# Relu-squared attention and a GELU feed-forward in one kernel: fourteen output stores issued by ScalarE instead of SyncE, one more gate on GpSimd, and a new instruction order in the middle

## The chip, the cores and the metric

The kernel runs on one core of one Trainium2 chip. The metric is the device time of one execution in microseconds (us). The core has TensorE (PE in the profile; PEld is its weight load), VectorE (DVE), ScalarE (ACT), GpSimd (POOL) and SyncE (SP), which work at the same time and wait for each other by semaphores. Transfers are issued from the queues of SP, ACT and POOL and carried out by 16 DMA engines.

## The reference

```python
B, H, S, D = 8, 12, 448, 64
scores = q @ k.transpose(0, 1, 3, 2) / sqrt(D)        # per batch and head
attn   = maximum(scores, 0) ** 2 / S
x      = (attn @ v).transpose(0, 2, 1, 3).reshape(3584, 768)
h      = x @ w_in                                     # w_in  768 x 2048
g      = 0.5 * h * (1 + erf(h / sqrt(2)))
out    = g @ w_out                                    # w_out 2048 x 768
```

All inputs and the output are float32 in memory.

## The kernel before

**The work.** There are eight batches of 448 tokens. A batch goes through attention in three groups of four heads. For each group and each of seven blocks of keys there is one step: four matmuls for the scores (`ps`, L741, 64x64 tiles of the array), a relu with scaling to bf16 (L753 on ACT or L755 on DVE), and a square (L762 on DVE). After seven steps a set of 28 matmuls multiplies by v (`pav`, L802), and two copies bring the result to `xT` (L511 on DVE, L513 on ACT).

The feed-forward has two layers. The first (`psh`, L854) takes `xT` times `w_in`, six matmuls of 448 columns for 128 hidden units, then one GELU on ACT (L864). For the last three batches it is done in blocks with sums of blocks and fewer products (`pb`, L998, L1035, L1044). The second layer goes over groups of 256 tokens, numbered 0 to 13. Each group has seven products of eight matmuls of 384 columns (`pso`, L1171), which are put together on DVE and ACT (L1205, L511, L513) in two tiles `osb` of 128 x 768, the two halves of the group. Each half is written to memory by two DMA transfers (L1132), because the rows of the output are split over two places there. There are three `osb` buffers, three PSUM buffers for attention and two for the feed-forward.

**How q and k come in.** For batches 2 to 7, POOL loads k, q and v with a cast to bf16 (L546, L467, L564). SP then transposes q and k by DMA: nine transfers `DMA_TRANSPOSE` for each batch (L660), three for each group of heads: one of k and two of q. I call them T(b,0) to T(b,8) for batch b. The first score matmul of batch b needs T(b,0), T(b,1) and T(b,2). T(b,...) may be issued when the loads of batch b have landed and when the scores of batch b-2 are done, because there are two buffers. The loads of the next batch overwrite what the transposes read. So POOL holds them back with a "gate", a tiny copy that reads the transposed data (L701 and L709): a gate behind T(b,2), one behind T(b,6), then the load of v of batch b itself, a gate behind T(b,8), then six loads of k and q of batch b+1. The v load of the last batch stands right behind its six loads of k and q.

**What sets the order.** Every piece of work is registered with `Scheduler.add`, with the engines that can do it, its planned length and the pieces that it needs. The string `ORDER` (L83 to L163) then names the pieces one by one with a letter for the engine (P, A, D, G for POOL, S for SP) and the number of the piece. `Scheduler.place` sends them to their engines in that order, so `ORDER` fixes what each engine does and in which order. POOL's pieces also stand in the list `pool_q`, which is only followed for what `ORDER` leaves out; `ORDER` leaves out nothing here.

**The queues.** In the order of instructions, each DMA issued by SP or ACT takes the next of eight landing semaphores, in the order of `ORDER`. Before it is issued, its engine waits until the transfer eight places before it has landed, since that one had the same semaphore. SP carries both the transposes and the stores in one in-order queue. ACT issues two loads at the start and two small stores at the end.

The lines that the prediction's steps touch are: L660 (transposes, SP), L1132 (stores), L701, L709, L564 (gates and v load, POOL), L741 (scores), L802, L854, L998, L1171 (the other sets on PE), L864 and L753 (ACT), L1205 (DVE into `osb`).

Of the kernel before, what the change touches and what calls it, by code (L numbers as in the profile page):

```python
# [15 lines left out]
HC = NC // 2  # L16
HS = S // 2
# [76 lines left out]
A260 D182 D187 P263 D215 A211 D188 P261 G151 A205 P207 A264 P216 S230 G153 D206 D185 D224 A262  # L94
A217 P192 A208 G154 D193 D194 D209 D212 P247 D221 A248 P255 P143 D218 A256 P201 P225 A144 A226
G237 D202 D203 P265 D227 D380 S231 D386 S232 P245 S233 A266 P362 A246 P372 A363 P370 A373 A371
D390 D388 P356 P366 A357 P368 A367 P376 D389 A369 A377 P358 P364 D383 D381 A359 A365 P360 P350
A361 P354 A351 P288 P282 D387 D384 A355 A289 P294 P378 A295 P374 P276 S234 A379 G240 D283 D284
D382 G149 P279 A375 P291 D280 D385 S235 P348 P352 P285 A292 A277 A349 D296 D290 D286 D287 A353
P306 P303 S236 P392 P300 D393 A304 P342 P394 D395 P396 P398 D391 A307 D281 A343 P312 P315 G152  # L100
A397 A301 A313 G155 G242 D278 D293 D316 G269 P297 G270 D399 G271 G272 P327 P400 D298 P402 D314
D302 D427 P324 A299 A328 S408 P309 D401 D403 P336 P404 A325 S409 A310 A337 P431 D305 D317 D326
G273 P318 A432 P339 P333 P435 D428 A334 G274 S410 D405 D311 P433 S411 S406 A340 P447 D319 A448
D344 D308 P462 D320 P321 G417 D434 P330 D429 P437 A322 A436 D329 D430 D335 A331 D341 P439 A323
S412 D338 D332 S413 P459 A463 P453 P345 A454 D460 D438 D440 S414 S415 P474 P465 D475 D455 G420
P441 P443 D442 A346 A466 P486 D444 A347 D467 G275 S416 P450 D451 A487 P456 D452 P531 G423 A532
D570 P547 A548 P549 P545 A550 D457 D571 S407 A546 P498 D464 P489 P504 D449 P529 D461 P523 A499
A490 P477 G418 D458 P480 D505 D478 A530 G419 P468 S551 G421 S552 A481 P471 A524 D476 D482 D469
D472 P483 D572 D473 P527 A484 S445 D488 P537 A528 P533 D506 P510 G422 D485 A470 A538 D491 A534
P507 P501 S553 D500 A511 G424 P539 A502 A508 G425 S554 P519 P625 G560 A626 P513 D479 A520 P492  # L110
P495 D514 D512 S555 P616 S556 S557 A540 D493 D515 P525 D496 A617 A494 G563 P535 P619 S558 D509
A526 D627 G426 S559 P613 A536 D614 G566 P610 P543 A544 D615 P541 D503 P521 D497 D573 G561 P640
A620 A611 P646 A641 D647 P516 D517 P634 A522 A542 D642 S446 P628 P574 A635 D629 P576 G562 P670
D612 S714 D621 D630 A518 S715 G564 P622 D618 G565 A575 P664 A623 A671 P578 D577 P580 P661 P637
A665 D624 D581 A638 P631 P649 D662 P676 A579 S716 D639 P582 P584 A632 D633 P652 A677 D583 A650
P667 D636 A653 D585 S588 D651 S717 D648 A668 D654 P643 A644 G567 P586 S718 D590 P594 P779 D645
D587 P673 P655 A780 G568 D592 D591 A595 P658 A674 P596 P782 D666 A659 S589 S719 D597 P773 A783
P598 A774 P600 D656 S720 P815 D663 P785 D675 A599 D657 P776 D669 D672 A786 G723 A777 A816 D601
G726 D660 D775 P602 D678 P604 P809 D735 D593 P791 S721 D603 D605 P679 A810 P806 P606 S722 D781
A680 S608 D778 P692 D607 D681 D792 A807 G569 A693 P706 P788 D787 P797 P824 A707 P686 A687 P704  # L120
D789 D790 G729 P702 D784 G724 P830 A798 S877 D793 A825 D817 P812 P794 G725 D831 A705 P803 A813
A795 D804 P836 D805 S878 S609 A703 G727 G728 A837 P708 A796 S879 D814 S880 P712 P833 D808 P839
D811 D733 P800 A709 P682 D801 A713 D802 D826 D799 A834 S881 A683 P700 G730 G731 D840 P696 A701
P688 S882 P925 P934 A935 P818 A689 D926 A697 P922 D832 P821 A819 P694 D734 D736 D923 D841 A820
G886 A695 A822 P710 S883 A711 D823 P827 P940 D828 G889 P931 D835 D829 P698 S884 A941 A699 D838
P690 A932 P684 D927 P919 G732 A691 P928 A685 D920 P842 D924 D936 A929 S885 P916 A843 A917 P949
P737 G892 G887 P739 D930 A950 P955 G888 D921 D844 S988 P943 S989 D933 G890 G891 A738 A956 D740
D918 D944 P964 P741 P743 A742 P745 D744 A965 D942 D746 P747 P749 P952 D753 D951 P946 S990 D748
# [4 lines left out]
P865 A1001 P849 A866 A1037 P857 P1006 D972 P1024 D1002 A850 D969 P985 A1025 P1009 D1007 A858 P1012  # L133
D1077 P875 P869 A876 P861 A1013 S996 D897 A870 D986 A862 P873 D899 A874 A987 D1038 D1010 P847 S771
P1057 A848 P1030 P1003 D1008 D1011 A1031 P853 D1069 D1058 A1004 P863 D1014 P1063 D1029 D1005 A864
P1018 P1021 A854 D1064 P1045 P859 A1022 A1019 D1032 D1073 A860 D1074 P845 P867 P1039 D1070 A1046
A846 A1020 D1023 D1078 A868 P1051 P1033 P851 A1034 D1035 A852 A1040 P902 D1026 D1047 P900 A1052
D1065 P1048 A901 D1041 D1053 D1059 P1060 A1061 D903 P1042 P1054 A1043 A1049 D1079 D1080 P904 A905
D1044 D1071 P906 D1062 A1055 P908 P1081 D1151 D907 S772 D909 D1056 P1083 P1098 A1099 P1100 D1076
P912 P910 D1149 D1150 A1082 D1050 P1066 D913 D911 S914 D1084 S915 P1085 D1072 D1101 P1153 A1067  # L140
A1068 P1102 A1154 D1075 P1087 D1152 P1104 A1086 D1189 P1089 A1103 D1190 P1106 D1088 P1155 D1105
D1090 P1092 D1107 A1091 D1191 P1109 A1108 D1156 P1095 P1112 D1093 P1115 D1110 A1094 P1132 D1096
A1111 P1117 D1113 A1097 P1134 D1192 A1116 A1133 P1157 A1114 D1118 P1119 D1135 P1136 A1158 P1121
P1138 A1120 P1123 A1137 P1140 D1122 P1159 D1139 D1124 P1126 D1141 A1125 P1143 A1142 D1160 P1129
P1146 D1127 P1161 D1144 A1128 D1130 A1145 P1163 D1147 A1131 D1301 A1148 D1162 D1302 P1165 D1169
D1164 S1167 P1173 D1170 D1166 S1168 P1175 D1171 D1174 P1177 D1172 D1176 D1303 P1179 D1304 A1178
P1181 D1180 P1183 D1263 D1182 P1185 D1261 D1184 S1187 P1193 D1262 P1210 D1186 S1188 P1195 D1264
P1212 A1194 A1211 P1265 D1196 P1197 D1213 P1214 A1266 P1199 P1216 A1198 P1201 A1215 P1218 D1200
P1267 D1217 D1202 P1204 D1219 A1203 P1221 A1220 D1268 P1207 P1224 D1205 P1227 D1222 A1206 P1244
D1208 A1223 P1229 D1225 A1209 P1246 A1228 A1245 P1269 A1226 D1230 P1231 D1247 P1248 A1270 P1233  # L150
P1250 A1232 P1235 A1249 P1252 D1234 P1271 D1251 D1236 P1238 D1253 A1237 P1255 A1254 D1272 P1241
P1258 D1239 P1273 D1256 A1240 D1242 A1257 P1275 D1259 A1243 A1260 D1274 P1277 D1281 D1276 S1279
P1285 D1282 D1278 S1280 P1287 D1283 D1286 P1289 D1284 D1288 P1291 D1290 P1293 D1292 P1295 D1375
D1294 P1297 D1373 D1296 S1299 P1305 D1374 P1322 D1298 S1300 P1307 D1376 P1324 A1306 A1323 P1377
D1308 P1309 D1325 P1326 A1378 P1311 P1328 A1310 P1313 A1327 P1330 D1312 P1379 D1329 D1314 P1316
D1331 A1315 P1333 A1332 D1380 P1319 P1336 D1317 P1339 D1334 A1318 P1356 D1320 A1335 P1341 D1337
A1321 P1358 A1340 A1357 P1381 A1338 D1342 P1343 D1359 P1360 A1382 P1345 P1362 A1344 P1347 A1361
P1364 D1346 P1383 D1363 D1348 P1350 D1365 A1349 P1367 A1366 D1384 P1353 P1370 D1351 P1385 D1368
A1352 D1354 A1369 P1387 D1371 A1355 A1372 D1386 P1389 D1393 D1388 S1391 P1397 D1394 D1390 S1392
P1399 D1395 D1398 P1401 D1396 D1400 P1403 D1402 P1405 D1404 P1407 D1415 D1406 P1409 D1413 D1408  # L160
S1411 P1417 D1414 D1410 S1412 P1419 D1416 D1418 P1421 D1420 P1423 D1422 S1433 P1425 D1424 P1427
D1426 S1434 P1429 D1428 S1435 P1430 D1431 S1436 D1432 S1437
# [232 lines left out]
def kernel(  # L395
# [300 lines left out]
    def add_gate(b, g):  # L696
# [438 lines left out]
    def add_group(g):  # L1135
# [79 lines left out]
        def store(x, c, queues):  # L1215
            return lambda e: store_rows(rows[x][0] // 128, osb(x), c, queues)
# [295 lines left out]
```

## Time and profile before

| what | value |
|---|---|
| device time, median of 3 runs (range) | 368.6 us (368.53 to 369.44) |
| device time of the profiled execution | 368.77 us |
| span of the profiled execution, first to last instruction | 367.0 us |
| granted TensorE clock | 0.998 |
| PE busy | 356.0 us, 97% |
| DVE busy | 286.4 us, 78% |
| ACT busy | 201.5 us, 55% |
| POOL busy | 63.7 us, 17% |
| DMA traffic | 47.25 MB |

The profiled execution took 1.8 us more than its span, which is time before its first and after its last instruction. Between 30 us and 250 us, PE is busy 217.64 of 220 us, ACT 142.08 and DVE 184.17. The chain that ended last goes by engine through PE for 80%, DMA for 8%, SP's queue for 5% and ACT for 4%.

How to read what follows: a line of a timeline has the start, the length, the engine, the line of the kernel and the operation, the tile that it writes and the tiles that it reads, the count, and in brackets the idle time of the engine before it and what ended that. "SPq" is SP's own queue: the time of such a line is the issue of a transfer, not the transfer. "us to landing" runs from the issue to the last byte's notice. In the chain of waits, each row is one stretch with its start, its length and who held the end up.

### The profile page before, as it was taken

The page shows a single profiled execution, that of the slowest core. Times are in us where ns is not written, and L with a number is a line of the kernel's source. Part 1 is how long each engine was busy: PE and PEld are TensorE (multiplying, and loading weights), DVE is VectorE, ACT ScalarE, POOL GpSimd, SP SyncE. Part 2 cuts the span into 40 slices and gives each one's busy share as a digit, 9 for nine tenths or more (in the row PEclk, how much of TensorE's full clock was granted, in tenths as well). Part 3 has the DMA queues.
Part 4 walks back from the last instruction along what each step waited for, and adds up shares of the span by engine and source line. Part 5 has one row for each costly group of instructions (what it writes and reads, how often), then busy time and mean ns, then how long its engine had stood idle before and what let it go on. Part 6 is the DMA issues. An engine that isn't in the chain of part 4 may idle for free.

```text
span 367.0 us, 8384 instructions
## 1 busy us (share of the span) xinstructions
PE 356.0 (97%) x3517; PEld 218.4 (60%) x3517; DVE 286.4 (78%) x480; ACT 201.5 (55%) x319; POOL 63.7 (17%) x103
## 2 busy tenths in 40 slices
PE   7899999999999899999999999999999999999995
PEld 3566465455544455554455544467886897688663
DVE  3998886389899787888997798799778558755863
ACT  4997754676757576748672656763540353045200
POOL 8665700160140240150150000000000000000000
PEclk9999999999999999999999999999999999999999
DMA  9999999999999999999899950002002301210232
GB/s 169 199 202 204 202 204 179 189 171 204 173 169 207 161 180 193 187 182 201 167 179 163 235 127 2 0 2 70 18 2 88 86 2 36 94 46 0 87 87 86
DMA packets 89700, 47.25 MB, mean 129 GB/s; under 512 B 55360, under 2 KB 86336, under 8 KB 89664
## 3 DMA queue, kind: packets, MB, share of 16 engines
q0 software_dynamic: 32912, 22.47, 42.0%
q1 hardware_dynamic: 56112, 23.76, 33.4%
q8 instruction: 27, 0.44, 0.5%
q10 hardware_dynamic: 640, 0.51, 0.4%
q14 instruction: 9, 0.07, 0.1%
HBM read 45.61 MB, written 11.01 MB: 154 GB/s over the span
## 4 chain that ended last, share of the span: by engine, by line
PE 80%; DMA 8%; SPq 5%; ACT 4%; issue 1%; DVE 1%; DVEq 0%; POOLq 0%; POOL 0%; ACTq 0%
PE pso L1171 32%; PE psh L854 20%; PE pb L998 13%; PE ps L741 8%; PE pav L802 7%; DMA qT<-nq 5%; SPq L660 4%; ACT a_sq L753 3%; DMA nk<-in_k_dram 2%; DMA k<-in_k_dram 1%; SPq L1132 0%; PE tp L605 0%; ACT kT L513 0%; ACT xT L513 0%; DVE a_sq L762 0%
## 5 line engine op out<-in xcount | busy, mean ns | idle before, releaser
L753 ACT ACTIVATE a_sq<-ps 128x896 bf16<-128x896 f32 (+1 forms) x122 | 106.8, 921 | 31.4 <-PE ps L741 31.1
L762 DVE TENSOR_TENSOR a_sq<-a_sq 128x896 bf16<-128x896 bf16 (+1 forms) x169 | 96.4, 614 | 2.8 <-ACT a_sq L753 2.4
L854 PE MATMUL psh<-xT,win_sb 128*128 128x448 bf16 (+1 forms) x516 | 95.7, 340 | 0.0
L854 PEld LDWEIGHTS <-win_sb 128*128 128x128 bf16 x516 | 48.2, 98 | 45.1 <-issue 8.9
L755 DVE TENSOR_SCALAR a_sq<-ps 128x896 bf16<-128x896 f32 (+1 forms) x47 | 50.6, 1076 | 20.6 <-PE ps L741 20.6
L1171 PEld LDWEIGHTS <-s_sb 128*128 128x128 bf16 x456 | 43.4, 98 | 29.9 <-issue 3.5
L864 ACT ACTIVATE h_sb<-psh 128x448 bf16<-128x448 f32 x80 | 43.3, 547 | 30.6 <-PE psh L854 30.4
L741 PE MATMUL ps<-qT,kT 64*64 64x448 bf16 (+1 forms) x756 | 47.6, 336 | 3.9 <-DMA qT<-nq 1.9
L1035 DVE TENSOR_TENSOR part<-pb,part 128x448 f32<-128x448 f32 x60 | 34.7, 619 | 21.0 <-PE pb L998 21.0
L1171 PEld LDWEIGHTS <-h_sb 128*128 128x128 bf16 x336 | 32.0, 98 | 23.2 <-issue 3.5
L1171 PE MATMUL pso<-wout_sb,h_sb 128*128 128x384 bf16 x224 | 41.1, 326 | 0.0
L1171 PE MATMUL pso<-wout_sb,s_sb 128*128 128x384 bf16 (+2 forms) x232 | 41.1, 321 | 0.0
L1171 PE MATMUL pso<-t_sb,s_sb 128*128 128x384 bf16 x224 | 41.0, 326 | 0.0
L802 PE MATMUL pav<-a_sq,v_sb 64*64 64x448 bf16 (+1 forms) x756 | 36.6, 329 | 0.3 <-ACT a_sq L753 0.2
L1205 DVE TENSOR_TENSOR osb<-pso,p_sb 128x384 f32<-128x384 f32 x42 | 23.3, 554 | 15.2 <-PE pso L1171 11.2
L741 PEld LDWEIGHTS <-kT 64*64 64x64 bf16 x756 | 18.4, 105 | 25.3 <-issue 19.9
L1044 ACT ACTIVATE h_sb<-part 128x448 bf16<-128x448 f32 x36 | 20.1, 578 | 20.2 <-DVE part L1035 19.9
L998 PEld LDWEIGHTS <-win_sb 128*128 128x128 bf16 x288 | 27.6, 98 | 2.3 <-issue 0.4
L802 PEld LDWEIGHTS <-v_sb 64*64 64x64 bf16 x756 | 21.5, 107 | 11.3 <-issue 1.2
L513 ACT CAST xT<-pav 128x448 bf16<-128x448 f32 (+1 forms) x31 | 15.3, 509 | 11.5 <-PE pav L802 9.8
L998 PEld LDWEIGHTS <-ws 128*128 128x128 bf16 x216 | 20.7, 98 | 0.0
L1171 PE MATMUL pso<-t_sb,h_sb 128*128 128x384 bf16 x112 | 20.5, 326 | 0.0
(60 smaller groups left out, 264.7 us busy)
## 6 DMA issues: line engine op xcount, KB each, us to landing
nk<-in_k_dram POOLq DMA_DIRECT2D x23, 224.0 KB, 8.5
nq<-in_q_dram POOLq DMA_DIRECT2D x21, 224.0 KB, 9.3
v_sb<-in_v_dram POOLq DMA_DIRECT2D x5, 672.0 KB, 10.0
out_dram<-osb SPq DMA_DIRECT2D x7, 336.0 KB, 3.6
v_sb<-in_v_dram POOLq DMA_DIRECT2D x9, 224.0 KB, 8.0
out_dram<-osb SPq DMA_DIRECT2D x7, 288.0 KB, 3.3
out_dram<-osb SPq DMA_DIRECT2D x8, 240.0 KB, 3.1
win_sb<-in_moe_w_in_dram POOLq DMA_DIRECT2D x8, 192.0 KB, 8.5
```

The source lines that it names most:

```text
L741: nc.tensor.matmul(ps[64 * j : 64 * j + 64, e, x * w : x * w + w], kT[r, g, i * 128 + 64 * j : i * 128 + 64 * j + 64], moving, start=True, ...
L753: A.activation(ar, ps, AF.Relu, scale=c_att)
L755: V.tensor_scalar(ar, ps, c_att, 0.0, op0=mybir.AluOpType.mult, op1=mybir.AluOpType.max,)
L762: V.tensor_mul(box["a2"][:, :, :used], ar, ar)
L802: nc.tensor.matmul(pav[0][o2 : o2 + 64, e, :w], vt[b][r, 2 * g + e, bass.ts(i, D)], box["a2"][r, y, o : o + w], start=(i == 0), stop=(i == ...
L854: nc.tensor.matmul(ph[:, x * n : x * n + n], win_sb[:, kd, bass.ts(m + x, 128)], xT[b][:, kd, c], start=(kd == 0), stop=(kd == KD - 1),)
L864: A.activation(h_ring()[:, m : m + nm, o + c.start : o + c.stop], box[0][:, :S].rearrange("p (x n) -> p x n", x=nm), AF.Gelu,)
L998: nc.tensor.matmul(bank[name][:, y, z * HS : z * HS + HS], w[:, k, bass.ts(mm, 128)], right()[:, k], start=first and k == 0 and z == 0, st ...
L1035: V.tensor_add(get(to), ps(name), get(other))
L1044: A.activation(h_ring()[:, m : m + 2, o + half[c].start : o + half[c].stop], src().rearrange("p (x n) -> p x n", x=2), AF.Gelu,)
L1171: nc.tensor.matmul(box[bank][:, n0:n1], left()[:, kf], right()[:, kf, n0:n1], start=bool(need) and kf == 0, stop=kf == K2 - 1, skip_group_ ...
L1205: V.tensor_add(out()[:, n0:n1], box[bank][:, n0:n1], other()[:, n0:n1])
```

## The change

There are three edits. First, the stores of groups 0 to 6 of the second layer (two halves of two transfers each, 28 transfers) are registered for ACT and issued on ACT's queue; the stores of groups 7 to 13 stay on SP. Second, a function `add_vgate` registers a small copy on POOL that reads transposed q of batch 7 and needs T(7,5); it is registered last, as piece 1441. Third, `ORDER` is new from batch 1's attention to the blocks of batch 5 (the first 72 entries of PE and its last 124 are the same). The number of pieces of each kind stays the same on PE. ACT has 14 store pieces more, two relus fewer and five copies fewer; DVE has these seven more.

```diff
+ACT_STORES = 7
...
-A260 D182 D187 P263 D215 A211 D188 P261 G151 A205 P207 A264 P216 S230 G153 D206 D185 D224 A262
+D224 D215 G151 P247 A260 A211 A248 D187 P265 A205 P192 D182 P216 D185 P207 D217 A266 P245 D206
...
-D953 P937 D750 A947 G893 D954 P982 P958 D754 P757 A758 P759 P761 D957 S751 S991 D938 A959 A983
-P997 A939 D960 P973 A998 D755 P979 G894 D760 D948 S992 P763 A762 A974 P765 D966 D764 D999 P767
-P967 S752 S993 D756 D766 D945 P976 A980 S994 A977 D975 D968 P961 P1015 A1016 P1027 D768 D896 D1028
-P769 D770 P871 D962 S995 G895 P855 D898 D981 D978 A872 A963 P970 D971 A856 D1017 P1036 D984 P1000
...
+D918 P745 G891 D923 A950 D753 P743 D924 D744 G893 P958 P982 A947 A959 G894 G895 P937 P979 D983
+P976 D754 A977 D938 A980 D746 S990 P747 D748 A939 P749 S991 D948 D750 P757 D755 P952 P1003 S992
+D960 S993 S994 A758 A752 P943 A1004 P759 D942 D756 D953 P761 D760 P763 A762 D984 D764 D978 P765
...
+D975 A860 A1016 A1034 G1441 S996 P964 P869 D965 D966 P847 P1009 P1030 D969 D1014 A1010 P985 D1031
...
+    def add_vgate(b):
+
+        def fn(e):
+            nc.gpsimd.tensor_copy(gate, get_T(b)[0][:, 32 * KC : 32 * KC + 16])
+
+        pool_q.append(sch.add((("POOL", 0.2, 0.3),), fn, [Tq[b, 1, 1][0]]))
...
         if g < NG - 1:
-            sch.add((("SP", 0.6, 2.8),), store(1, full, [nc.sync] * 2), [c22, c21], frees=("osb",))
-            sch.add((("SP", 0.6, 2.8),), store(0, full, [nc.sync] * 2), [c11] + c12, frees=("osb",))
+            queue, eng = (nc.scalar, "ACT") if g < ACT_STORES else (nc.sync, "SP")
+            sch.add(((eng, 1.0, 2.8),), store(1, full, [queue] * 2), [c22, c21], frees=("osb",))
+            sch.add(((eng, 1.0, 2.8),), store(0, full, [queue] * 2), [c11] + c12, frees=("osb",))
...
+    add_vgate(B - 1)
     sch.run({"PE": pe_q, "POOL": pool_q})
```

In these lines S988 to S996 are T(7,0) to T(7,8), G893 and G894 the last loads of k and q of batch 7, G895 its load of v, G1441 the new gate, S751 and S752 the two stores of group 4, the second of which becomes A752.

More of the change, by code (lines that the diff above doesn't have):

```diff
@@ L99 @@
[L99 to L128, printed above, removed]
@@ L159 @@
[L159 to L162, printed above, removed]
+D224 D215 G151 P247 A260 A211 A248 D187 P265 A205 P192 D182 P216 D185 P207 D217 A266 P245 D206
+P263 A193 S230 A208 D209 A246 P255 G153 A264 D218 D221 P261 D194 G154 A256 A262 D188 P201 D212
@@ new lines @@
+S231 D380 S232 P225 P143 A202 A203 S233 D381 A226 A227 P376 A144 P370 S234 D383 A377 D388 P368
+G237 A371 G240 P358 A369 D384 P348 G149 D389 A359 A349 P378 P356 A379 A357 P372 A373 P362 A363
+G152 D386 D385 D387 P350 P360 A351 A361 G155 P364 P285 A365 P291 D292 P279 S235 A286 S236 P352
+P294 A280 P288 D390 A353 P276 A277 P354 P366 A355 P303 D295 D289 G242 A367 D287 P282 A283 P306
+P374 D296 P392 D281 D278 G269 A304 A375 G270 P330 P318 D307 P342 A393 P394 A319 D391 A343 P396
+P336 G271 D284 S408 D293 D305 D290 A331 D395 P309 S409 G272 P297 D337 P312 S410 A310 D382 A298
@@ new lines @@
+D397 P300 P398 D332 A299 A301 D320 D311 S411 A313 G273 D344 P400 D399 P315 S412 D427 A316 P333
+G274 P324 D401 P402 D314 P404 A325 D403 P431 A406 D302 D317 D308 P327 D428 P321 S413 D432 D405
+A328 D429 D322 P339 P433 G417 S414 D329 A334 A340 D341 A323 P462 G420 G275 S415 P465 S416 D335
+A463 D326 A466 G423 P453 D434 A454 D464 D338 D430 P435 G418 P437 P459 P450 P345 D438 D460 D436
+P456 A451 G419 S551 P483 A346 D484 P439 P441 P474 D347 A457 P495 D440 P447 D452 D572 A496 P443
+P480 D475 D442 D444 A448 D455 P471 P504 P529 A472 D485 D458 D461 G421 P545 A530 P525 A505 G422
@@ new lines @@
+A546 D467 P547 P477 S552 D449 P468 A481 P501 D506 S553 A526 D478 A548 D570 D476 A445 D502 P486
+P539 A469 D479 D487 G424 P531 A540 A532 P535 D497 A407 P549 P489 P510 S554 A536 D470 G425 D488
+P498 S555 P533 D503 A550 D511 D499 D482 A534 P519 S556 A490 P537 D473 D491 A520 P507 P492 A538
+D508 D509 P513 P622 P521 A514 G560 S557 D512 A623 P527 A522 D493 G563 D500 S558 A494 P610 P652
+D515 S559 A528 A611 P516 D571 G426 D612 P625 G566 A653 D624 D626 P543 A544 P523 P541 A517 A524
+A542 G561 A518 D627 P574 D575 P576 G562 D577 P619 P640 P616 A620 S714 D617 A641 G564 P578 P628
@@ new lines @@
+P613 P649 P580 G565 S715 G567 D654 D629 A614 A650 S716 D642 D581 D621 P634 G568 D630 D651 A579
+P673 P646 D615 A446 S717 A647 D618 P582 A635 P584 D585 D583 P670 S718 A674 P631 P637 A671 S719
+P643 G723 D573 A638 A644 D636 D592 D590 D591 D648 D645 P594 S720 D639 P586 S721 D587 P676 A595
+A588 A677 A632 P598 P596 D593 P661 A633 A662 P776 G726 P655 D678 D597 P788 D777 D599 D663 D789
+P791 P600 G569 A656 P602 D601 S722 P604 D672 A657 P785 D675 A792 D603 P667 P664 P606 G729 D668
+P658 G724 A786 D605 P782 A665 P779 D607 G725 D793 D787 A608 G727 P696 D783 A659 A697 P712 D669
@@ new lines @@
+A780 P688 A713 D666 P824 D660 D825 P773 P679 P812 A689 P694 G728 D781 A813 D778 A695 P706 D680
+P684 P797 A774 A707 P815 D681 P800 S877 D784 A685 S878 P702 S879 D735 D733 A816 A801 D826 D775
+D790 A703 D798 P698 P692 P806 P809 A693 G730 D802 D807 G731 A810 A699 P794 D817 P803 D808 D814
+P821 P710 A822 S880 D795 S881 P690 A711 D796 A804 G886 P925 A691 S882 S883 D799 P836 D811 A926
+P830 P708 D837 A589 D805 D734 P686 A831 P833 P827 A828 A687 P818 D834 A709 S884 G889 G732 P928
+S885 A609 A819 D832 D835 P839 D929 P700 P704 G892 P934 A840 D820 P970 D829 A701 G887 P919 A705
@@ new lines @@
+A1037 D1076 D1053 A866 P902 D1062 A901 P904 D1071 A1058 D1059 D1077 A1082 P1085 P1021 D1074 A772
+A1022 D903 D1038 P1066 P1024 P1098 A1067 P906 A905 A1025 D1078 D1023 D1068 D1075 D907 P908 P1083
+P1100 D1151 D1189 A1099 D1026 D1190 P1042 P910 D1149 D1084 P1102 D1101 D1043 D909 D1072 D1044 P912
+D911 D1150 P1089 P1087 P1104 A914 P1153 D913 D1152 A1103 P1106 A915 A1086 A1154 D1080 D1088 P1155
+D1105 D1090 P1092 D1107 A1091 D1191 P1109 A1108 D1156 P1095 P1112 D1093 P1115 D1110 A1094 P1132
+D1096 A1111 P1117 D1113 A1097 P1134 D1192 A1116 A1133 P1157 A1114 D1118 P1119 D1135 P1136 A1158
@@ new lines @@
+P1121 P1138 A1120 P1123 A1137 P1140 D1122 P1159 D1139 D1124 P1126 D1141 A1125 P1143 A1142 D1160
+P1129 P1146 D1127 P1161 D1144 A1128 D1130 A1145 P1163 D1147 A1131 D1301 A1148 D1162 D1302 P1165
+D1169 D1164 S1167 P1173 D1170 D1166 S1168 P1175 D1171 D1174 P1177 D1172 D1176 D1303 P1179 D1304
+A1178 P1181 D1180 P1183 D1263 D1182 P1185 D1261 D1184 S1187 P1193 D1262 P1210 D1186 S1188 P1195
+D1264 P1212 A1194 A1211 P1265 D1196 P1197 D1213 P1214 A1266 P1199 P1216 A1198 P1201 A1215 P1218
+D1200 P1267 D1217 D1202 P1204 D1219 A1203 P1221 A1220 D1268 P1207 P1224 D1205 P1227 D1222 A1206
@@ new lines @@
+P1244 D1208 A1223 P1229 D1225 A1209 P1246 A1228 A1245 P1269 A1226 D1230 P1231 D1247 P1248 A1270
+P1233 P1250 A1232 P1235 A1249 P1252 D1234 P1271 D1251 D1236 P1238 D1253 A1237 P1255 A1254 D1272
+P1241 P1258 D1239 P1273 D1256 A1240 D1242 A1257 P1275 D1259 A1243 A1260 D1274 P1277 D1281 D1276
+S1279 P1285 D1282 D1278 S1280 P1287 D1283 D1286 P1289 D1284 D1288 P1291 D1290 P1293 D1292 P1295
+D1375 D1294 P1297 D1373 D1296 S1299 P1305 D1374 P1322 D1298 S1300 P1307 D1376 P1324 A1306 A1323
+P1377 D1308 P1309 D1325 P1326 A1378 P1311 P1328 A1310 P1313 A1327 P1330 D1312 P1379 D1329 D1314
@@ new lines @@
+P1316 D1331 A1315 P1333 A1332 D1380 P1319 P1336 D1317 P1339 D1334 A1318 P1356 D1320 A1335 P1341
+D1337 A1321 P1358 A1340 A1357 P1381 A1338 D1342 P1343 D1359 P1360 A1382 P1345 P1362 A1344 P1347
+A1361 P1364 D1346 P1383 D1363 D1348 P1350 D1365 A1349 P1367 A1366 D1384 P1353 P1370 D1351 P1385
+D1368 A1352 D1354 A1369 P1387 D1371 A1355 A1372 D1386 P1389 D1393 D1388 S1391 P1397 D1394 D1390
+S1392 P1399 D1395 D1398 P1401 D1396 D1400 P1403 D1402 P1405 D1404 P1407 D1415 D1406 P1409 D1413
+D1408 S1411 P1417 D1414 D1410 S1412 P1419 D1416 D1418 P1421 D1420 P1423 D1422 S1433 P1425 D1424
@@ L163 @@
+P1427 D1426 S1434 P1429 D1428 S1435 P1430 D1431 S1436 D1432 S1437
 """
```

38 lines of the change are left out of this document (8 added, 30 removed).

## The prediction

> **What bounds the kernel now.** I read the page first, then the waits of PE, then PE's timeline at each gap, then the chain of waits and SP's and POOL's timelines there.
>
> ```profile
> span 367.0 us, 8384 instructions
> PE 356.0 (97%) x3517; PEld 218.4 (60%) x3517; DVE 286.4 (78%) x480; ACT 201.5 (55%) x319; POOL 63.7 (17%) x103
> PE   7899999999999899999999999999999999999995
> PE ps L741 <- DMA qT<-nq: 1.9, 2, 1.2
> PE ps L741 <- issue: 0.5, 1, 0.5
> ```
>
> PE is the bound, so a change pays only by PE's idle time or by less work on PE. PE's first 72 pieces keep their order, so the idle time before about 30 us stays. From 30 to 250 us PE is busy 217.64 of 220 us: 2.36 us idle. The two rows of waits (total, times, longest) make up all of it: two scores waited for transposes of q, 1.9 us, and one wait without a named releaser, 0.5 us. The third also ends just after a transpose of q has landed. PE's timeline shows the three:
>
> ```profile
> 121.19 0.57 PE L741 MATMUL ps<-qT,kT 64*64 64x448 bf16 x8 [1.25 <-DMA qT<-nq]
> 147.16 0.57 PE L741 MATMUL ps<-qT,kT 64*64 64x448 bf16 x8 [0.50 <-issue]
> 204.90 0.76 PE L741 MATMUL ps<-qT,kT 64*64 64x448 bf16 x12 [0.62 <-DMA qT<-nq]
> ```
>
> These are the first scores of batches 4, 5 and 7, each waiting for T(b,2). By issue plus time to landing T(4,2) landed at 121.06 (114.48 + 6.57), T(5,2) at 147.07 and T(7,2) at 204.76. What made the last one late is in SP's and POOL's timelines and the chain:
>
> ```profile
> 187.52 0.73 POOL L467 DMA_DIRECT2D nq<-in_q_dram  x1
> 188.25 0.85 POOL L564 DMA_DIRECT2D v_sb<-in_v_dram  x1
> ...
> 190.73 1.22 SPq L660 DMA_TRANSPOSE kT<-nk  x1
> 192.06 8.17 SPq L660 DMA_TRANSPOSE qT<-nq  x2
> 200.33 1.96 SPq L1132 DMA_DIRECT2D out_dram<-osb  x2
> ...
> 196.29 8.47 DMA qT<-nq
> ```
>
> The last q load lands at 198.32 (10.8 us after issue), v of batch 7 at 203.1 (14.8), and T(7,0) at 203.0. So the transposes came through only when the loads were out, and v cost them 4.8 us.
>
> **The change, part by part.**
>
> *PE's work.* In the order of instructions PE has the same matmuls, with one change more from attention to feed-forward and back. In the chain 16 `pso` matmuls take 2.60 us between like neighbours and 2.71 us beside scores, so a change costs about 0.11 us, both ways **+0.2 us**.
>
> *Stores leave SP.* Five stores stood among the transposes up to T(6,2): one in batch 3 (1.01 us on SP), one in batch 4 (1.19), two in batch 5 (0.78 and 0.96, plus 0.3 of waiting), one in batch 6 (0.97), with gaps some 5.5 us; those at 98.63, 125.89 and 158.74 stand behind a batch's last transpose and delay none. The chain is a loop: transposes, gates, loads, next transposes, so an advance carries on. Lower end: nothing, if the 16 engines and not SP set the pace of the transposes. Upper end: batch 2 had no store and went from its last load to T(2,8) in 9.95 us (65.02 to 74.97); batches 3 to 6 took 12.0, 11.4, 13.6 and 11.6, so 8.7 us. I take 5, near the issue time, since unhampered transposes land every 1.2 us and SP needs 1.25 to 1.33 for each issue. A rule of the Trainium skill (DMA: Bandwidth & Descriptors, "Issuing engines are not separate DMA queues") says that another issuing engine saves only sequencer time; by it the 5.5 us is a ceiling.
>
> *What PE asks for now.* Counting PE's pieces in the order of instructions up to the first score of each batch, against before: batch 4 two score steps (0.19 each), one `pav` set (1.32) and one change more, +1.8; batch 5 two `pso` sets (1.30) and three changes more, one step less, +2.7; batch 6 three steps less, -0.6; batch 7 two `pso` sets less, one step and three changes more, -2.1. From the old starts, less the stalls before them, PE is there at 121.7, 148.1, 174.7 and 200.4 us. T(4,2) and T(5,2) are early enough even at their old landings (121.06, 147.07): **-1.25 and -0.50**. T(6,2) landed at 176.11 and must gain 1.4, T(7,2) at 204.76 and must gain 4.4. With 5 both hold: **-0.62** and no new wait, batch 7 with 0.6 us to spare.
>
> *The gate on POOL.* POOL's order is: last k, last q, v of batch 7, then the new gate. Nothing stands behind it, so it holds v back from nothing and costs 0.2 us (gate rows: 0.21) on an idle engine. v still waits for the last `pav` of batch 5, on PE at 185.9 (186.19 before), plus 1.3: it is issued at about 187.5 and stays ahead of T(7,0). **Zero.**
>
> *Stores on ACT.* 28 issues. ACT's rows are 0.48 and 0.49 us for loads and 0.85 for two stores at the end, so about 0.95 a store, 13.3 us in all. ACT's queue is in order: behind a store stand relus and GELUs, and PE waits for these through its PSUM buffers. Seven fewer relus and copies give back 2 x 0.92 + 5 x 0.5 = 4.3 us, and DVE gets 2 x 1.08 + 5 x 0.55 = 4.9 us on 184.17 of 220. ACT is busy 142.08 of these 220 us, and it waits for PE before 49 GELUs, 30.4 us, or 0.62 each; one issue fits such a hole, two exceed it by 0.33, and the second PSUM buffer gives PE a set of 1.13 us more. Lower end 0; upper end 13.3, if none were hidden. No PE wait for ACT is longer than 0.4 us in the whole trace, which is the nearest row, so I take **+0.2**.
>
> Waits that come with it: an ACT store waits for `osb` and for the landing eight places before. In batch 6 that is T(6,0), T(6,3) and T(6,4), landed in the old trace at 172.2 to 178.0 and needed after 174; they come earlier. The one to watch is the late store of group 4: it stands on ACT where PE begins batch 7, waits for T(7,0), and group 5's second `osb` waits for that store's landing. It is on time exactly when T(7,2) is.
>
> Sum: -2.37 + 0.2 + 0.2 = -2.0 us. Against the profiled execution, 368.77 (span 367.0 and 1.8 around it), that is 366.8; on the median of the runs, 368.6, it is **366.6 us**.
>
> **Rivals.**
>
> 1. *Batch 7 is late.* v is not moved behind the transposes, PE wants batch 7 4.4 us earlier, and the advance may be less than 5. The time is 366.6 + (4.4 - advance). With 2.2 us it is 368.8: no change. With none it is 371.0: slower; it is slower from an advance under 1.2. For it: the DMA share is 0.98 to 1.12 in the stretches of the transposes (1.31 at most elsewhere), and the stores' bytes still go through the same engines. Against it: four batches with stores took 1.4 to 3.6 us longer than batch 2.
>
> 2. *ACT is held at its issues* and the result is slower. Place: nine of the 14 ACT stores stand between transposes. SP's transposes take 1.25 us to issue, up to 4.1 when the engines are full. If an ACT issue had to wait for the one in progress, a store would cost 2 x 1.25 = 2.5 us more; less the hole of 0.62 and the buffer's 1.13 that leaves 0.75 for PE, nine times 6.8: 373.4. It decides from about 0.9 us of waiting per issue; half the waits give 370. Against it: at 0.74 us SP and ACT issue at once:
>
> ```profile
> 0.74 0.39 SPq L1285 DMA_DIRECT2D q<-in_q_dram  x1
> 0.74 0.48 ACTq L1284 DMA_DIRECT2D k<-in_k_dram  x1
> 1.25 0.49 ACTq L1287 DMA_DIRECT2D k<-in_k_dram  x1
> ```
>
> The ACT issue beside SP's takes 0.48, the one alone 0.49. The Trainium skill (Perfetto Trace Analysis, "DMA Instruction — HWDGE (DVE, Sync)") says that the descriptor generator is shared by two sequencers and locked by one at a time; by that rule this rival holds, and these two rows speak against it, though neither has a transpose.
>
> 3. *Small costs add up*: two to four ACT stores or DVE's seven extra pieces each hold PE by 0.5 us, which eats 1 to 2 us of the gain: 367.6 to 368.6, no change.
>
> **How the numbers follow.** A measurement of this kernel can tell 0.3%, 1.1 us, from no change: faster is under 367.5, slower over 369.7. Forecast (advance over 3.5, ACT covered): 0.57. Batch 7 half late: 0.17, no change. Small costs: 0.08, no change. Batch 7 with no advance: 0.08, slower. ACT held: 0.10, slower. So faster 0.57, no change 0.25, slower 0.18. The range goes from 365.9 (the sum without ACT's 0.2, and up to 0.5 of small gaps gone) to 370.4 (batch 7 with almost no advance, or ACT held by half): that leaves out the top of rivals 1 and 2.
>
> **What would show it.** Right: no gap of PE at the first scores of batches 4, 5, 6 and 7; the transposes of a batch issued without a break in some 10 us; T(7,2) landed before 200.4; ACT's issues at 0.4 to 0.5 us; no `osb` row of DVE that waits for a DMA. Wrong: a PE gap in front of batch 7's first score, with v landing just before T(7,0) (rival 1); ACT issues over 1 us and PE waiting for `a_sq` or `h_sb` (rival 2); many short PE waits for ACT or DVE between 80 and 250 us (rival 3).

## The result and the profile after

The changed kernel takes **375.0 us** (median of 4 runs, 374.55 to 375.87) against 368.6 for the kernel before: ratio 1.0171, interval 1.0147 to 1.0195. That is slower, and outside the range that was forecast (366.6 us; 365.9 to 370.4). The profiled execution took 375.87 us with a span of 374.0. Medians and ratios here are those of the fast executions; the one slow one, of `pool_gate`, is left out. The lines from the scores on (L741 before) have numbers 8 higher in `after` and 6 higher in most of the experiments; of the lines shown ahead of them, those that both kernels have moved by one at most.

The page of the kernel after: the span, PE's busy time, and PE in 40 slices of 9.35 us.

```profile
span 374.0 us, 8378 instructions
...
PE 357.6 (96%) x3517; PEld 218.8 (59%) x3517; DVE 290.7 (78%) x487; ACT 196.9 (53%) x312; POOL 64.5 (17%) x104
...
PE   7899999998898898999999999999999999999995
```

There are holes between 84 and 150 us that the kernel before did not have (slices 10, 11, 13, 14 and 16). The waits of PE, with the total, the times and the longest in us:

```profile
PE ps L749 <- ACT a_sq L761: 4.7, 5, 3.3
PE psh L862 <- ACT h_sb L872: 3.2, 2, 1.7
...
PE pav L810 <- ACT a_sq L761: 0.6, 2, 0.4
```

The three waits of before for transposes of q at batches 4, 5 and 7 (2.37 us) are down to one of 0.5 us; the forecast had none. In their place PE now waits for ACT. From 30 to 250 us PE stands idle 7.92 us, before 2.36. Over the whole span it is idle 5.4 us longer and busy 1.6 us longer with as many matmuls (357.6 against 356.0): together the 7.0 us of span. What does ACT wait for? The waits of ACT:

```profile
ACT a_sq L761 <- DMA qT<-nq: 8.9, 2, 6.5
...
ACT h_sb L872 <- DMA qT<-nq: 3.9, 1, 3.9
```

The relu of a score (`a_sq`) and a GELU (`h_sb`) read PSUM and need no transposed q. ACT's timeline from 84 to 99 us shows what stands in front of it:

```profile
86.06 1.73 ACT L761 ACTIVATE a_sq<-ps 128x896 bf16<-128x896 f32 x2 [0.74 <-PE ps L749]
91.16 3.11 ACTq L1140 DMA_DIRECT2D out_dram<-osb  x2
94.32 2.54 ACT L761 ACTIVATE a_sq<-ps 128x896 bf16<-128x896 f32 x3 [6.53 <-DMA qT<-nq]
```

and PE's at the same place:

```profile
95.29 0.38 PE L749 MATMUL ps<-qT,kT 64*64 64x448 bf16 x4 [3.25 <-ACT a_sq L761]
```

The store is the second half of group 0. Its two transfers were issued at 91.16 and 93.93 us; the issues themselves take 0.37 and 0.34 us. The records carry the number of the landing semaphore, and the trace has the landings. Put side by side for three stores on ACT:

| store, half and transfer | semaphore last used by | that landed at | store issued at |
|---|---|---|---|
| group 0, second half, first | T(3,1), issued 85.00 | 91.08 | 91.16 |
| same, second | T(3,2), issued 86.86 | 93.91 | 93.93 |
| group 1, second half, first | T(4,1), issued 110.27 | 116.40 | 116.48 |
| same, second | T(4,2), issued 111.93 | 117.30 | 117.32 |
| group 0, first half, second | T(4,4), issued 116.66 | 122.70 | 122.72 |

Each transfer goes out 0.02 to 0.08 us after the landing of a transpose that SP had issued 5 to 7 us earlier. In the kernel before, the stores and the transposes went through SP's queue in one order, and a store's number came from eight transfers back in that queue.

In `after` the numbers are handed out so that all nine transposes of a batch come ahead of a store that stands among them: T(3,0) to T(3,8) have numbers 4, 5, 6, 7, 0, 1, 2, 3, 4, the store has 5 and 6, T(4,0) has 7. Eight places back from the store is T(3,1), although in `ORDER` the store stands between T(3,4) and T(3,5).

### The profile page after: what moved, and what is told of

Read it like the earlier page. It is cut to its first block, busy times and chain, and to the rows that moved or that the text cites. A ratio compares the mean times of both kernels' runs of the same rounds, so it can differ in the third digit from the quotient of the medians.

```text
span 374.0 us, 8378 instructions
## 1 busy us (share of the span) xinstructions
PE 357.6 (96%) x3517; PEld 218.8 (59%) x3517; DVE 290.7 (78%) x487; ACT 196.9 (53%) x312; POOL 64.5 (17%) x104
## 4 chain that ended last, share of the span: by engine, by line
PE 47%; DMA 31%; SPq 14%; POOL 3%; issue 3%; ACT 0%; DVE 0%; ACTq 0%; POOLq 0%; DVEq 0%
PE pso L1179 25%; SPq L661 14%; DMA nq<-in_q_dram 13%; PE pb L1006 13%; DMA qT<-nq 8%; PE psh L862 5%; DMA win_sb<-in_moe_w_in_dram 3%; DMA v_sb<-in_v_dram 3%; PE pav L810 3%; PE ps L749 2%; DMA wout_sb<-in_moe_w_out_dram 2%; DMA nk<-in_k_dram 2%; POOL nk L547 1%; DMA kT<-nk 1%; POOL v_sb L565 1%
## 5 line engine op out<-in xcount | busy, mean ns | idle before, releaser
L761 ACT ACTIVATE a_sq<-ps 128x896 bf16<-128x896 f32 (+1 forms) x120 | 104.9, 921 | 42.7 <-PE ps L749 25.6
L763 DVE TENSOR_SCALAR a_sq<-ps 128x896 bf16<-128x896 f32 (+1 forms) x49 | 52.6, 1077 | 22.5 <-PE ps L749 21.9
L749 PEld LDWEIGHTS <-kT 64*64 64x64 bf16 x756 | 19.5, 105 | 28.4 <-issue 22.4
L1213 DVE TENSOR_TENSOR osb<-pso,p_sb 128x384 f32<-128x384 f32 x42 | 23.3, 555 | 11.6 <-PE pso L1179 9.0
## 6 DMA issues: line engine op xcount, KB each, us to landing
wout_sb<-in_moe_w_out_dram POOLq DMA_DIRECT2D x4, 384.0 KB, 12.4
```

Of the source, the lines that this page charges most:

```text
L749: nc.tensor.matmul(ps[64 * j : 64 * j + 64, e, x * w : x * w + w], kT[r, g, i * 128 + 64 * j : i * 128 + 64 * j + 64], moving, start=True, ...
L761: A.activation(ar, ps, AF.Relu, scale=c_att)
L763: V.tensor_scalar(ar, ps, c_att, 0.0, op0=mybir.AluOpType.mult, op1=mybir.AluOpType.max,)
L1213: V.tensor_add(out()[:, n0:n1], box[bank][:, n0:n1], other()[:, n0:n1])
```

## The experiments

**Theory A**: ACT is held by landing semaphores that its stores share with SP's transposes. **Rivals**: B, the new order itself costs the time; C, the bytes of the stores do, whoever issues them; later D, ACT's waits and the lateness of the transposes are two limits side by side. The results in one table: time, ratio to the kernel before with its interval, PE's idle time from 80 to 250 us, the landing of T(7,2), and the mean time from the landing of T(b,0) to that of T(b,8) over batches 3 to 6, all us. The last three columns are of one profiled execution each. The ratio is to executions of the kernel before in the same session, whose medians were 368.2 to 368.6, so it is not the quotient of the medians shown.

| kernel | median | ratio (interval) | PE idle | T(7,2) | T(b,0) to T(b,8) |
|---|---|---|---|---|---|
| before | 368.6 | 1 | 2.4 | 204.8 | 11.6 |
| after | 375.0 | 1.0171 (1.0147 to 1.0195) | 7.9 | 209.4 | 12.4 |
| order_alone | 384.0 | 1.0461 (1.0400 to 1.0522) | 12.5 | 214.9 | 15.6 |
| stores_alone | 382.7 | 1.0408 (1.0362 to 1.0453) | 11.3 | 201.5 | 11.7 |
| no_stores | 367.1 | 0.9975 (0.9954 to 0.9996) | 0.0 | 192.9 | 10.6 |
| one_row | 370.6 | 1.0061 (1.0036 to 1.0087) | 3.1 | 193.1 | 10.8 |
| pool_stores | 376.0 | 1.0206 (1.0149 to 1.0263) | 8.2 | 208.5 | 11.4 |
| pool_gate | 371.6 | 1.0076 (1.0044 to 1.0108) | 3.4 | 203.3 | 10.9 |
| first_on_sp | 376.1 | 1.0225 (1.0188 to 1.0262) | 6.2 | 208.7 | 12.5 |
| gate_after | 376.6 | 1.0232 (1.0162 to 1.0301) | 5.8 | 200.9 | 12.2 |
| gate_before | 367.45 | 0.9986 (0.9963 to 1.0010) | 0.3 | 200.0 | 11.7 |
| gate_again | 367.2 | 0.9962 (0.9939 to 0.9984) | 0.4 | 200.0 | 11.7 |
| behind_gate | 367.6 | 0.9999 (0.9979 to 1.0020) | 2.3 | 203.3 | 11.2 |
| stores_apart | 394.4 | 1.0709 (1.0676 to 1.0741) | 21.5 | 214.9 | 12.2 |

### The two halves of the change by themselves

```diff
 order_alone
-ACT_STORES = 7
+ACT_STORES = 0
-ORDER: A406 A407 A445 ... A915   (14 stores)
+ORDER: S406 S407 S445 ... S915   (same places)
```

> The changed kernel with its new order, but with the 14 stores of groups 0 to 6 issued by SP again, at the same places. Theory A (an ACT store waits for the landing of a transpose that SP has only just issued, because the landing semaphores are handed out to all nine transposes of a batch ahead of the store, and ACT's relus and GELUs stand behind it): on SP the stores take their numbers in SP's own order, eight transfers back, so ACT's waits on transposes of q (8.9 and 3.9 us) and PE's waits for a_sq and h_sb go; PE keeps at most a late batch 6 and 7 (1.4 and 3.0 us, because the order asks for them earlier): 368 to 371 us. Rival B (the new order itself costs the time, by what it puts on ACT and DVE): PE's waits for a_sq and h_sb stay and the time is 374 to 375.

Measured 384.0: worse than either forecast. ACT's waits are gone, so they do come from the issuer and rival B falls as it stood; but PE now waits 10.1 us for transposes, with one gap of 7.27. PE's timeline there:

```profile
192.14 0.96 PE L747 MATMUL ps<-qT,kT 64*64 64x448 bf16 x8 [7.27 <-DMA qT<-nq]
```

SP's timeline ahead of it, with a store and then T(6,7) and T(6,8):

```profile
179.54 1.00 SPq L1138 DMA_DIRECT2D out_dram<-osb  x2
180.59 3.15 SPq L659 DMA_TRANSPOSE qT<-nq  x2
```

and POOL's, with the load of v of batch 6:

```profile
181.78 0.83 POOL L563 DMA_DIRECT2D v_sb<-in_v_dram  x1 [0.24 <-issue]
```

The store takes 1.0 us of SP, and T(6,8) is issued at 181.92, just behind the load of v at 181.78. T(6,7), issued at 180.59, landed after 3.7 us; T(6,8) landed at 192.00, after 10.1 us, with v (191.66). So a store on SP can cost more than its 1.0 us of issue, if it is what puts a transpose behind a load; here that is read from the trace, and no run moves this store alone.

```diff
 stores_alone (order of before)
-ORDER: S406 S407 S445 ... S915
+ORDER: A406 A407 A445 ... A915
```

> The order of before, with the 14 stores of groups 0 to 6 issued by ACT at the same places; v of batch 7 as before. Theory A: the semaphores are again handed out to a batch's transposes ahead of the store, ACT is held for 2 to 6 us at several stores that stand among transposes, and PE loses 3 to 7 us in gaps that wait for a_sq or h_sb: 371 to 376. Rival B (the order): ACT's issues cost nothing, the three gaps of before go or stay: 366.5 to 369.

Measured 382.7, above theory A's range but in its way. The waits of PE:

```profile
PE psh L860 <- ACT h_sb L870: 7.0, 1, 7.0
PE ps L747 <- ACT a_sq L759: 5.6, 6, 4.0
```

Both long gaps stand behind ACT stores that went out 0.02 to 0.08 us after landings: at 114.71 and 115.54 us behind T(4,1) and T(4,2), at 143.56 and 144.26 us behind T(5,1) and T(5,2).

The new order is better for stores on ACT by some 8 us than the old one, and worse by 15 for stores on SP. Neither half works alone.

### Without the stores, and without their bytes

```diff
 no_stores
 def store(x, c, queues):
+    if g < ACT_STORES:
+        return lambda e: None
     return lambda e: store_rows(...)
```

> The changed kernel without the stores of groups 0 to 6, so that half of the output is not written. It shows the ceiling of the change: no issue and no wait on ACT or SP, no bytes of these stores. Theory A: no PE gap over 0.4 us that waits for a_sq or h_sb between 80 and 200 us; 366 to 368. If SP's slots and the store's bytes were what lengthens the transposes, a batch goes from its last load to its last transpose in about 10 us, as batch 2 did (9.95); if the transposes are paced by the engines' own work, in 11.5 to 14 us as now, and batch 7 is late by 2 to 4 us. Rival B (order): 373 to 375 all the same.

367.1. The windows of PE (stretch, length, busy, clock, DMA share, GB/s) have no idle time left:

```profile
80.00:120.00 40.00, 40.00 (x384) 1.00 1.22 171
120.00:160.00 40.00, 40.00 (x388) 1.00 1.15 167
160.00:200.00 40.00, 40.00 (x408) 1.00 1.23 168
```

T(7,2) lands 12 us earlier than before. From its 551st matmul, at about 30 us, to its last, PE takes 331.4 us, before 333.7: 2.3 less. So without these stores the order takes all of PE's gaps away, as the forecast said. The time, however, fell by only 0.9 us (0.1 to 1.7), less than the forecast's 2.0: in the profiled execution the 551st matmul came 1.1 us later than in that of before (30.19 against 29.11). Over the profiled executions of this document it comes at 28.6 to 30.4 us, with the same pieces ahead of it; why is not shown.

```diff
 one_row
+    r = 1 if t < 2 * ACT_STORES else m
-    queue.pop(0).dma_start(to[k, p0 : p0 + m, c], src[y : y + m, c])
+    queue.pop(0).dma_start(to[k, p0 : p0 + r, c], src[y : y + r, c])
```

> The changed kernel, but every store of groups 0 to 6 moves one row and not 16 to 112, so that most of that half of the output is not written. All issues, places and semaphores stay, the bytes go. Theory A: ACT still issues a store at the moment when a transpose that SP issued two or three places before has landed; with the transposes some 10% quicker (10.8 to 11.5 us a batch, as without any stores) the waits are shorter but stay: 3 to 6 us of PE gaps for a_sq and h_sb, 370 to 374. Rival C (the bytes): no gap, 367.

370.6, as theory A said. The transposes go as quickly as without stores (10.8 against 10.6 us a batch), so the bytes had slowed them, not the number of issues. ACT still waits: the first transfer goes out at 90.98, T(3,1) had landed at 90.90. So of the 7.9 us between `after` and `no_stores`, 3.5 remain with waits and issues alone, and 4.4 come with the bytes.

### Stores on POOL

```diff
 pool_stores
-queue, eng = (nc.scalar, "ACT") if g < ACT_STORES else (nc.sync, "SP")
+queue, eng = (nc.gpsimd, "POOL") if g < ACT_STORES else (nc.sync, "SP")
-ORDER: A406 A407 ... A915
+ORDER: G406 G407 ... G915   (G445, G407, G589 and G609 behind a batch's loads; G608 between two loads)
```

> The changed kernel with its order on PE, ACT, DVE and SP, but with the 14 stores of groups 0 to 6 issued by POOL, whose transfers have landing semaphores of their own; bytes as before, four of the stores stand a few pieces earlier or later so that no load waits behind one. Theory A (the landing semaphores shared by ACT's stores and SP's transposes hold ACT): no wait of ACT on transposes of q, PE's gaps for a_sq and h_sb from 80 to 200 us go from about 7.9 us to under 1, and the time is 367 to 369. Rival C (the stores' bytes in the engines, whoever issues them, slow the transposes and so PE): a batch still takes 12 to 14.7 us from its last load to its last transpose, batch 7 is late by 2 us or more, and the time is 370 to 374.

Half of theory A came true: no ACT wait for transposes, no PE wait for `a_sq` over 0.4 us. But the time is 376.0. PE waits at other places, for the transposes themselves. Its waits:

```profile
PE ps L747 <- DMA qT<-nq: 8.2, 4, 3.4
PE ps L747 <- ACT a_sq L759: 1.4, 5, 0.4
```

and two of the four in PE's timeline:

```profile
178.01 0.76 PE L747 MATMUL ps<-qT,kT 64*64 64x448 bf16 x12 [2.27 <-DMA qT<-nq]
...
208.68 0.57 PE L747 MATMUL ps<-qT,kT 64*64 64x448 bf16 x8 [3.41 <-DMA qT<-nq]
```

These are batches 6 and 7. So theory A explains where PE stands in `after`, but to take ACT's waits away did not make the kernel faster: with ACT free, PE comes to batch 6 in time and the transposes are late. That is theory D. It is not a clean test of D, for POOL's loads and stores share eight semaphores too (numbers 99 to 106). The last load of q of batch 6 waited for the landing of v of batch 5 at 162.79, with G608 issued shortly before it:

```profile
163.07 0.73 POOL L466 DMA_DIRECT2D nq<-in_q_dram  x1 [2.29 <-DMA v_sb<-in_v_dram]
```

In the kernel before, these loads followed each other without such a wait. So part of the 2.27 us at batch 6 may be this kernel's own; how much is not shown.

```diff
 pool_gate: as pool_stores, and
-ORDER: ... G895 (v of batch 7) ... G1441 (gate) ...
+ORDER: ... G1441 G895 ...
```

> As the kernel before this one in the list (stores on POOL), and v of batch 7 behind the copy that waits for T(7,5), so that it is really issued behind the transposes. Expected: T(7,0) to T(7,5) land 2 to 6 us earlier against the last load of batch 7 than with v ahead; if batch 7's first score does not wait in the other kernel, the time is the same within 0.3%; if it waits there, that wait goes. v then lands some 10 us after T(7,5), before its first pav.

371.6: 4 us less than `pool_stores`. T(7,2) landed at 203.3 instead of 208.5, 3.8 us behind the last load instead of 6.8, and the gap at batch 7 is gone; v landed at 225.1.

```diff
 first_on_sp
+queue1, eng1 = (nc.sync, "SP") if g == 0 else (queue, eng)
-sch.add(((eng, 1.0, 2.8),), store(1, full, [queue] * 2), ...)
+sch.add(((eng1, 1.0, 2.8),), store(1, full, [queue1] * 2), ...)
-ORDER: A406
+ORDER: S406
```

> The changed kernel with one of its 14 early stores, the second half of group 0, put back on SP at the same place; the other 13 stay on ACT. On ACT it waited for T(3,1) and T(3,2) and PE lost 3.25 us at 95 us. Theory A: that wait of ACT and that gap go, the ones at 118 to 124 and at 148 us stay. Theory D, formed from the runs so far (ACT's waits and the late transposes of batches 6 and 7 are two limits side by side, and while ACT holds PE the transposes catch up): the time falls by less than 3.25, to 372 to 375, and waits for transposes at batches 5 to 7 come up by what is missing. Without D: 371.8.

The gap at 95 us went, a wait of 1.5 us for transposes came at batch 7, and the time is 376.1: nothing gained from 3.25 us of PE's idle time. The trace shows where it went. PE's idle time from 80 to 250 us fell by 1.7 us only (7.92 to 6.22): besides batch 7, the wait for `h_sb` at 117 us is 3.06 us long instead of 1.51. Behind that wait PE's granted clock is at one half for 3.41 us, in which PE is busy throughout; by an estimate from these two figures that costs 1.7 us more. The windows there (clock behind the count of matmuls):

```profile
117.00:118.00 1.00, 1.00 (x6) 0.76 2.28 183
118.00:119.00 1.00, 1.00 (x5) 0.50 0.25 23
120.00:121.00 1.00, 1.00 (x13) 0.54 1.11 362
```

So D's direction is seen (1.0 us more at batch 7), and the clock makes up about as much as all waits that came back; in the profiled execution of `after` it stayed at 1.00 there. The gap at 95 us was no fixed price either: in `gate_after`, below, whose edit touches nothing before 190 us, T(3,1) landed 1.4 us earlier, there is no such gap, and the one at 117 us is 3.45 us long.

### v of batch 7 behind its transposes

`gate_after` swaps G895 and G1441 in the changed kernel, `gate_before` (and `gate_again`, the same code) has the old order with stores on SP and the copy that waits for T(7,5) put in ahead of v.

> The changed kernel with one edit: the load of v of batch 7 stands behind the copy that waits for T(7,5) on POOL, not ahead of it. T(7,2) lands 4 to 6 us before 209.35; only the gap of 0.48 us at batch 7's first score can go, ACT's waits stay: 374.5, the same within 0.3%.

> The kernel before, stores on SP, with one change: POOL's copy that waits for T(7,5) stands ahead of the load of v of batch 7, so v is issued behind the transposes and not at 188 us. Theory (v of batch 7 costs the transposes of batch 7 up to 4.8 us, and PE waits 0.62 us for them): T(7,2) lands 2 to 5 us before 204.8, the gap at batch 7's first score goes, v lands at about 215 to 222, and the time is 368.0, if v is not needed before that. Rival: the first pav of batch 7 then waits for v and the time is 369 to 372. Rival: the transposes of batch 7 are late by their q loads alone and nothing changes, 368.6.

> The kernel before with v of batch 7 behind the gate, a second time with more rounds, to tell whether it is faster at all: 0.9986 with an interval over 1 in the first run. Expected 0.997 to 0.999, from the one gap of 0.62 us at batch 7's first score.

POOL's timeline of `gate_again` shows v really held back, 18 us later than before:

```profile
206.19 0.20 POOL L708 COPY gate<-qT 128x16 bf16<-128x16 bf16 x1 [18.63 <-DMA qT<-nq]
206.64 0.84 POOL L563 DMA_DIRECT2D v_sb<-in_v_dram  x1 [0.26 <-issue]
```

T(7,2) lands at 200.0, 4.8 us earlier than before; v lands at 216.2, early enough. In the old order this measured 0.9962 (0.9939 to 0.9984), after 0.9986 with an interval over 1 in the first measurement: a small gain, clear of none in one measurement of two. In the changed kernel T(7,2) came 8.5 us earlier and the time did not fall (376.6): only 0.48 us of PE had hung on it, and there too the clock was at one half for 3.41 us, behind the gap of 3.45 us at 117 us.

```diff
 behind_gate: as gate_before, and three stores moved on SP
-ORDER: S445 among S551..S559; S589 among S714..S722; S609 among S877..S885
+ORDER: S559 S445; S722 S589; S885 S609
```

> The kernel before, all stores on SP, v of batch 7 behind the gate, and the three stores that stood among the transposes of batches 4, 5 and 6 without being needed soon (groups 1 and 2, and 3) moved behind the last transpose of the batch on SP. If a store's bytes among the transposes cost the next transpose about 2 us (3.1 against 1.15 between two landings), T(4,2) lands at about 118.7 and T(6,2) at about 173.5, the last PE gaps of 0.5 us go, and the time is 366.5 to 367.5, 0.3 to 0.5% under the kernel before. Rival: the bytes only move into the next load phase, and the time is that of the gate alone, 367.5 to 368.3.

0.9999 (0.9979 to 1.0020): no gain over the gate alone, nor over the kernel before. The profiled execution took 369.69 us, one of the longest of twelve. In it T(4,2) still landed 3.2 us after T(4,0), without a store between, so there that pause was not the store's; what makes it is open.

### The numbers, not the place

```diff
 stores_apart: eight stores at other places of ACT's order
-ORDER: A406 behind T(3,4), A445 and A407 behind T(4,2), A446 behind T(5,2) ...
+ORDER: A406 behind T(3,6), A445 behind T(4,6), A407 behind T(4,7), A446 behind T(4,8) ...
```

> The changed kernel with eight of the ACT stores moved to other places in the order, where their data is long ready and fewer transposes are on the way: the second half of group 0 some 4 us later, both halves of groups 1 and 0 to the end of batch 4's transposes, the others by up to 18 us later or earlier. If ACT were held by the store's data, by SP's issues or by the engines, this would help: 370 to 373. Theory A: what counts is the order in which the landing numbers are handed out, and there the late store of group 0 now comes eight places behind T(5,1), so it waits on ACT, with all relus and GELUs behind it, from about 124 us until T(5,1) has landed, at 140 to 146 us. PE stands still for 10 to 20 us there and the time is 380 to 395.

394.4. ACT's timeline at the first half of group 0:

```profile
126.24 0.55 ACT L512 CAST xT<-pav 128x448 bf16<-128x448 f32 x1
140.28 0.96 ACTq L1138 DMA_DIRECT2D out_dram<-osb  x2
141.29 0.54 ACT L870 ACTIVATE h_sb<-psh 128x448 bf16<-128x448 f32 x1 [14.50 <-issue]
```

and PE's:

```profile
142.70 0.59 PE L747 MATMUL ps<-qT,kT 64*64 64x448 bf16 x4 [14.15 <-ACT a_sq L759]
```

T(5,1) landed at 140.26, the store went out at 140.28, on a semaphore that T(5,1) had used. The data had been ready for over 25 us. A later place made it worse by the number that it got. This is the strongest evidence for theory A's mechanism, since the place and the size of the wait were said beforehand. A second gap of PE, 6.88 us long and over at 188.88, was not forecast, but is of the same kind: two later stores went out at 182.48 and 187.43, 0.08 us after the landings of T(6,2) and T(6,4), whose numbers they had. The numbers do not follow one simple rule: here A406, which `ORDER` has behind T(3,6), has the two numbers on either side of T(4,2).

## Why the prediction was wrong

**What bounds the kernel**: right. PE's three gaps were all that the order could gain on PE, and in `no_stores` they are gone: 2.3 us in PE's work behind 30 us, though only 0.9 us (0.1 to 1.7) in the time.

**Waits that come with it**: this step failed. It said that an ACT store waits for the landing eight places before, counted in `ORDER`, and found T(6,0), T(6,3) and T(6,4), landed by then. The description ahead of the prediction says the same. The waiting itself is as it said, and in the kernel before, where SP issued all stores, the numbers do follow `ORDER`. For ACT's stores they run in another sequence: in `after`, all nine transposes of a batch first. Which rule makes that sequence is not shown by the runs; the numbers in the instruction records are. The step also looked at batch 6, while the waits that hurt were in batches 3, 4 and 5. **Stores on ACT**, taken at +0.2, is the term of the sum that it spoilt: the PE gaps over 0.4 us that wait for ACT come to 7.4 us. That no PE wait for ACT exceeded 0.4 us in the old trace was no bound, since ACT issued nothing among the transposes there. The issues were sized rightly (0.32 to 0.61 us each, one 0.81).

**Stores leave SP**: an advance of 5 us was taken; its lower end, nothing, held. T(6,2) landed at 175.9 us, before at 176.1, and from T(b,0) to T(b,8) the transposes took 12.4 us a batch (before 11.6) although five stores had left SP. The row that would have told is one that the trace of before could not show: with one-row stores, at the same places, they take 10.8, and T(6,2) lands at 167.8, though ACT's waits stay. So the stores' bytes, not SP's issues, had held the transposes back. The rule cited there (DMA: Bandwidth & Descriptors of the Trainium skill, "Issuing engines are not separate DMA queues") agrees: it should have been read as the likely case and not as a ceiling.

**What PE asks for now**: right. It had PE at batch 6 at 174.7 us and at batch 7 at 200.4. In `pool_stores`, where ACT holds nothing, PE is there at 174.5 and 200.5, when its stalls up to then are taken off. T(6,2) landed at 177.9 and T(7,2) at 208.5, later than in the kernel before (176.1 and 204.8), perhaps in part by POOL's own wait. So rival 1's mechanism is what PE met once ACT's waits were gone. In `after` it shows as 0.5 us only, because PE was already over 7 us late.

**The gate on POOL**: right in the cost, since v was issued at 196.31, 17 us ahead of the gate, when the last `pav` of batch 5 (on PE at 194.5) allowed it. The time and the order were off: forecast were 187.5 us and a place ahead of T(7,0), but with PE late v came behind T(7,0) and T(7,1) and just ahead of T(7,2), at 197.48. v landed at 208.84 and T(7,2) at 209.35; with v behind it (`gate_after`) T(7,2) landed at 200.9.

**Rivals.** Rival 2 had the place and nearly the price (ACT held among the transposes, 373.4) but another cause, and so was given 0.10. ACT's issues did not lengthen: at 118.38 one took 0.81 us within an SP issue that ran from 118.30 to 122.03. The rule on the shared descriptor generator (Trainium skill, Perfetto Trace Analysis, "DMA Instruction — HWDGE (DVE, Sync)") is not borne out as a hold of ACT for as long as SP's issue lasts. Nor did the prediction see that rivals 1 and 2 do not add up: while ACT holds PE, late transposes cost little, and the other way round. To take away one of them, or a part, gained nothing in three kernels (`pool_stores` 376.0, `gate_after` 376.6, `first_on_sp` 376.1); to take away the bytes did (`one_row` 370.6).

What stays open: how much of the 4.4 us of the bytes goes through ACT's waits, how much of the late transposes in `pool_stores` is POOL's own wait, and why `no_stores` gained less in time than on PE.

## What to carry to other kernels

Before a DMA is moved to another engine's queue, read the landing semaphore that it gets there and when its last user lands: an engine in the critical loop stands behind that wait with all its work. If transposes or loads are paced by bytes, another issuer buys only the issue slot; a load issued just ahead of them can cost more than the slot. To hold such a load back (v of batch 7, which the change itself did not do) was the one edit here on the kernel before that measured faster, by 0.4% and 0.1% in two measurements, the second not clear of none. Where two late chains end at the same engine, take both away in one experiment before judging either.

## What the runs showed of the hardware

In these traces a transpose issued just after the load of v landed with it: T(6,8) of `order_alone` after 10.1 us, issued 0.14 us behind v, against 3.7 for the transpose before it. T(7,0) of the kernel before, issued 2.5 us behind v, landed after 12.3 us, 0.05 us ahead of v; with v held back (`gate_again`) it took 7.0.

Long idle stretches of PE cost more than themselves here. The windows of `stores_apart` around the 14.15 us gap (columns as above, PE's clock is the fourth number):

```profile
126.00:130.00 4.00, 2.55 (x40) 1.00 1.14 197
130.00:133.00 3.00, 0.00 (x0) 0.94 1.30 217
133.00:134.00 1.00, 0.00 (x0) 0.50 1.31 197
...
142.00:146.00 4.00, 3.30 (x12) 0.50 1.07 192
146.00:150.00 4.00, 4.00 (x24) 0.96 1.32 181
```

PE stopped at 128.6; some 4 us later the granted clock was 0.50, and it stayed there for about 3.5 us after PE was busy again. After the gaps of 3.25 us (`after`) and 3.41 us (`pool_stores`) it stayed at 1.00; after those of 3.06 us (`first_on_sp`), 3.45 us (`gate_after`) and 4.04 us (`stores_alone`) it fell. So no fixed length of a gap decides it. Between 80 and 250 us the stretches at one half are 3.41, 6.83 or 13.65 us long in all five kernels that have them, once, twice or four times 3.41. The Trainium skill (TensorE: Matmul & The Clock Gate, "What's actually happening") gives about 3.4 us of idleness and as long of work for the two steps. The lengths of the stretches agree with it; as a limit for the gap the figure does not hold here, with 3.06 us enough in one run and 3.41 us not in another. Part of what `stores_alone`, `order_alone`, `stores_apart`, `first_on_sp` and `gate_after` lost is this clock, not waiting.
